# Block products from tile 6 on, the transposed rows of tiles 4 and 5 by way of HBM, and a new written order, in an attention and MLP kernel

## The chip, the cores and the metric

The kernel runs on one core of a Trainium2 chip. Its time is the device time of one execution in microseconds (us). Three runs of the kernel before took 357.02, 357.13 and 357.69 us; the median is 357.13 us.

## The reference

Two stages follow one another. The first is attention over 4 batches, 8 heads, 768 positions of width 64; each query sees the keys less than 16 positions away and, of every block of 32 keys, one summary (the maximum of the keys, the mean of the values):

```python
k_sum = k.reshape(B, H, nb, 32, D).max(axis=3)
v_sum = v.reshape(B, H, nb, 32, D).mean(axis=3)
scores_l = where(abs(i - j) < 16, scale * q @ k.T, -1e9)
scores_s = scale * q @ k_sum.T + log(32)
a = softmax(concat(scores_l, scores_s))
x = a @ concat(v, v_sum)
```

The second works on the 3072 rows of x, with 512 inputs and 1024 hidden values:

```python
h = x @ w_in
solu = h * softmax(h)
ln = (solu - mean) / sqrt(var + 1e-6) * g_ln
out = ln @ w_out
```

## The kernel before

The 3072 rows are 24 tiles of 128. A tile of the second stage needs its attention first, in which the query windows of two neighbouring tiles share loads. Each tile then runs through these steps, many of which stand side by side in the program for different tiles:

- TensorE (PE) makes scores `s`; VectorE (DVE) adds the mask and takes the maximum (L695), ScalarE (ACT) takes the exponential `e` and its sum `z` (L707), adds 1e-9 to `z` (L714), DVE inverts it (L716), and `e<-e,z` multiplies (POOL at L381 or DVE at L380). PE transposes `e` and makes `x` (L796).
- A matrix product in full precision is three products of rounded halves: high by low, low by high, high by high. So `x` is split into `xh` and `xl`, the weights in advance as well.
- `first(t)` (L935) makes `h`: 8 pieces of 3 matmuls of 128x512 for a tile (L949). `first_two(t)` (L960) makes `h` of two tiles at once with seven block products in the place of eight: 7 products of 2 pieces of 3 matmuls, 42 for the pair (L968). It needs combinations of the weights (`ws`, made once) and of the rows of x (`sums`, `combine` in L841 and the lines behind it). The constant `PAIRED` is the first tile that goes this way; `SUMS` and `GATE` are the tiles at which the weights' combinations begin and from which they may.
- The normalised rows `he` have to be transposed for the last product. `turn(t)`: tiles below `FAR_FROM` go through PE (16 transposes `lt<-ident,he`, L739, then a copy and a subtraction from PSUM, L1122); tiles from `FAR_FROM` on are transposed within blocks by DVE (L1074), sent to HBM by one DMA (`farl<-tbl`, L1078), and read back by four (`lt<-farl`, L1084), all issued by SyncE (SP); then `lh` (a cast) and `ll` (a subtraction) are made from SBUF.
- `second(t)` makes `o` with 24 matmuls (L1144); ACT or DVE scales it (L1152, L1154) into `os`, and ACT issues the store (L1156).

The order of the whole program is written out: `Plan` numbers every operation, and the list `ORDER` says in which order they are issued; each engine takes its own in that order. Some operations may run on several engines, with a cost each; the table `OTHERS` (in `Plan`) names those that do not run on their first engine. Costs and landing times give each operation a planned start. These decide one thing only, since the order is fixed: where the plan has PE waiting within the first 80 us, matmuls of a tile of zeros are put in (`keep_up` and `idle`, L1337), called fillers here:

```python
for o in order:
    if o.engine == "pe":
        while at + self.SYNC < min(o.start + o.late, self.FILL):
            at += self.keep_up(at, done)
```

Of the kernel before, what the change touches and what calls it, by code (L numbers as in the profile page):

```python
# [1381 lines left out]
```

## Time and profile before

| | us |
|---|---|
| median of three runs | 357.13 |
| the profiled execution | 357.58 |
| its span, first to last instruction | 355.9 |
| PE busy | 348.6 (98%) |
| DVE busy | 289.7 (81%) |
| ACT busy | 257.3 (72%) |
| POOL busy | 211.4 (59%) |

The mean granted clock of TensorE is 0.997 of the full one. The busy share is an average over the span; a stage in which DVE is busy all the time and one in which it is idle lie behind the 81%. A matmul's row shows the length of one instruction, which overlaps the next; what one costs in a row of them is the length of the row divided by their number.

### The profile page before, as it was taken

To read this page: it belongs to the slowest core of one execution; us is meant where nothing else is said; L and a number is where in the kernel's file an instruction comes from. 1 tells how busy PE (TensorE), PEld (TensorE's weight loads), DVE (VectorE), ACT (ScalarE), POOL (GpSimd) and SP (SyncE) were. 2 spreads that over 40 slices of the span, in tenths; PEclk is the share of its full clock that TensorE was granted. 3 is DMA by queue.
4 is the path that set the end of the run, shared out by engine and by line. 5 is a ranking of instruction groups with operands and counts; after the bars stand their busy time and mean duration, and the time that the engine had idled before them with its cause. 6 is when DMAs were issued, how large, how long until landed. Compare 5 with 4: busy or idle time off the path is not lost.

```text
span 355.9 us, 9340 instructions
## 1 busy us (share of the span) xinstructions
PE 348.6 (98%) x3298; PEld 273.1 (77%) x3298; DVE 289.7 (81%) x960; ACT 257.3 (72%) x773; POOL 211.4 (59%) x342
## 2 busy tenths in 40 slices
PE   7899999999999999999999999999999999999995
PEld 3356576777878887788888888888887888888884
DVE  3999999997888989899798977978988787967220
ACT  3888899974987768668879867785985975736311
POOL 5616558795978777876567277374457373422460
PEclk9999999999999999999999999999999999999998
DMA  7999979047006356285495775375274434355512
GB/s 252 409 409 409 330 288 329 11 136 271 33 3 220 92 196 228 77 266 161 122 361 155 225 246 178 123 228 191 97 240 125 157 116 174 132 172 181 173 60 89
DMA packets 28530, 68.19 MB, mean 192 GB/s; under 512 B 3852, under 2 KB 13324, under 8 KB 26948
## 3 DMA queue, kind: packets, MB, share of 16 engines
q1 hardware_dynamic: 24620, 60.87, 50.7%
q10 hardware_dynamic: 3864, 6.74, 5.2%
q8 instruction: 26, 0.43, 0.5%
q14 instruction: 20, 0.16, 0.1%
HBM read 49.55 MB, written 15.73 MB: 183 GB/s over the span
## 4 chain that ended last, share of the span: by engine, by line
PE 93%; DVE 3%; DMA 2%; SPq 0%; ACT 0%; POOL 0%; issue 0%; ACTq 0%
PE o L1144 38%; PE h L949 13%; PE hu L968 12%; PE x L796 7%; PE hl L968 6%; PE s L674 6%; PE t L739 4%; PE hf L968 3%; DMA kraw<-in_k 2%; PE x L1337 2%; PE vs_ps L561 2%; PE lt L739 1%; DVE e L695 1%; PE vs_ps L574 1%; PE x L788 1%; DVE ksum L541 1%
## 5 line engine op out<-in xcount | busy, mean ns | idle before, releaser
L1144 PE MATMUL o<-w,lh 128*128 128x512 f32 (+1 forms) x400 | 133.4, 388 | 0.0
L1144 PEld LDWEIGHTS o<-w,lh 128*128 128x128 f32 x400 | 74.0, 188 | 15.8 <-DVE he L1039 0.2
L707 ACT ACTIVATE e<-e,nm 128x120 f32<-128x120 f32 x192 | 73.2, 388 | 7.2 <-DVE nm L695 7.2
L1144 PE MATMUL o<-w,ll 128*128 128x512 f32 (+1 forms) x200 | 76.3, 382 | 0.0
L949 PE MATMUL h<-w,xh 128*128 128x512 f32 x128 | 44.9, 404 | 0.0
L695 DVE CUSTOM_DVE_ANT_0 e<-s,mask 128x120 f32<-128x120 f32 x192 | 40.7, 276 | 3.1 <-PE s L674 3.0
L381 POOL TENSOR_TENSOR ll<-lt,lh 128x512 fp32r<-128x512 f32 x19 | 26.7, 1405 | 27.8 <-ACT lh L373 14.7
L1144 PEld LDWEIGHTS o<-w,ll 128*128 128x128 f32 x200 | 37.6, 188 | 6.5
L707 ACT ACTIVATION_READ_ACCUMULATOR e<-e,nm 128x1 f32 x192 | 37.1, 193 | 0.0
L373 ACT COPY at<-t 120x512 f32<-120x512 f32 x40 | 22.0, 588 | 18.7 <-PE t L739 18.1
L381 POOL TENSOR_TENSOR e<-e,z 128x960 f32<-128x960 f32 (+1 forms) x16 | 28.2, 1765 | 8.1 <-DVE z L716 8.0
L1047 POOL TENSOR_SCALAR he<-he,nmu 128x512 f32<-128x512 f32 x24 | 19.2, 801 | 19.2 <-DVE nmu L1042 19.1
L1152 ACT ACTIVATE os<-o,y 128x512 f32<-128x512 f32 (+1 forms) x21 | 14.2, 676 | 21.9 <-PE o L1144 7.5
L949 PEld LDWEIGHTS h<-w,xh 128*128 128x128 f32 x128 | 24.0, 188 | 7.3 <-issue 1.7
L796 PEld LDWEIGHTS x<-at,vt 120*64 120x64 f32 (+1 forms) x768 | 24.3, 138 | 3.4 <-issue 1.8
L796 PE MATMUL x<-at,vt 120*64 120x64 f32 (+1 forms) x768 | 26.4, 224 | 0.0
L1054 ACT ACTIVATE sq<-he 128x1024 bf16<-128x1024 f32 x24 | 25.3, 1056 | 1.0 <-ACT z L714 0.8
L373 ACT CAST lh<-lt 128x512 fp32r<-128x512 f32 x37 | 21.5, 609 | 5.7 <-PE o L1144 5.7
L949 PE MATMUL h<-w,xl 128*128 128x512 f32 x64 | 25.0, 390 | 0.0
L381 POOL TENSOR_TENSOR xl<-sums,xh 128x256 fp32r<-128x256 f32 (+1 forms) x15 | 14.1, 937 | 16.4 <-DVE xh L374 9.2
L1074 DVE STREAM_TRANSPOSE tbl<-he 128x1024 f32<-128x1024 f32 x18 | 22.3, 1238 | 1.0 <-POOL he L1047 0.8
L1031 ACT ACTIVATE he<-hs,hm 128x512 f32<-128x512 f32 x24 | 17.2, 718 | 8.0 <-DVE hm L1021 7.9
(176 smaller groups left out, 837.0 us busy)
## 6 DMA issues: line engine op xcount, KB each, us to landing
vt<-in_v SPq DMA_DIRECT2D x12, 1024.0 KB
farl<-tbl SPq DMA_DIRECT2D x18, 512.0 KB
lt<-farl SPq DMA_DIRECT2D x72, 128.0 KB
kraw<-in_k SPq DMA_DIRECT2D x16, 400.0 KB
out<-os ACTq DMA_DIRECT2D x23, 256.0 KB
qt<-in_q SPq DMA_DIRECT2D x11, 512.0 KB
raw<-in_w_in SPq DMA_DIRECT2D x8, 512.0 KB
raw<-in_w_out SPq DMA_DIRECT2D x8, 512.0 KB
```

Source lines behind the costliest of these rows:

```text
L373: by = {act: lambda: nc.scalar.copy(out=to(), in_=of()), dve: lambda: nc.vector.tensor_copy(out=to(), in_=of()), pool: lambda: nc.gpsimd.t ...
L381: pool: lambda: nc.gpsimd.tensor_tensor(out=to(), in0=a(), in1=b(), op=kind)}
L674: nc.tensor.matmul(scs[i * each].ap[cu * QT:(cu + 1) * QT, j, c:c + ks.shape[-1]], qs.ap[ds, 2 * pp + i, u * QT:(u + 1) * QT], ks, start=T ...
L695: nc.vector.tensor_tensor_reduce(out=e.ap[:, n, :], in0=scs[i * each].ap[:, j, (2 * i + up) * KC:(2 * i + up + 1) * KC], in1=mask[:, mi, : ...
L707: nc.scalar.activation(out=e.ap[:, n, :], in_=e.ap[:, n, :], func=AF.Exp, bias=nm.ap[:, n:n + 1], scale=-1.0, accum_out=z.ap[:, n:n + 1])
L796: nc.tensor.matmul(xp()[j * D:(j + 1) * D, i, qs], vs.ap[:k, u, cs], at.ap[:k, u % 2, n[j] + u // 2, :], start=not apart, stop=not apart o ...
L949: nc.tensor.matmul(hp.ap, a.ap[:, c, ts], w.ap[:, i], start=(c == 0 and n == 0), stop=(c == NKC - 1 and n == 2))
L968: nc.tensor.matmul(to.ap, operand(y, n)[:, c], w(c).ap(i), start=first and c == 0 and k == 0, stop=c == 1 and k == 2, skip_group_check=True)
L1047: op(pool, 0.68, lambda sl=sl: nc.gpsimd.tensor_scalar(out=e.ap[:, sl], in0=e.ap[:, sl], scalar1=nmu.ap, scalar2=1.0, op0=ALU.add, op1=ALU ...
L1054: op(act, 1.05, lambda: nc.scalar.activation(out=sq.ap, in_=e.ap, func=AF.Square, accum_out=ss.ap), r=[e], w=[sq, ss])
L1074: op(dve, 1.17, lambda: nc.vector.transpose(out=tb.ap.rearrange("p (q c a) -> p q c a", q=4, a=32), in_=of().rearrange("p (c q a) -> p q c ...
L1144: nc.tensor.matmul(o.ap[:, cols], a.ap[:, f, :], w.ap[:, i, cols], start=(f == 0 and n == 0), stop=(f == NFC - 1 and n == 2))
```

## The change

- `PAIRED` goes from 8 to 6, so tiles 6 and 7 are a pair in `first_two`; `SUMS` and `GATE` go from 4 to 2, so the combined weights are begun after tile 2.
- `FAR_FROM` goes from 6 to 4: rows of tiles 4 and 5 go by way of HBM.
- Four kinds of small operations get further engines to choose from; some costs of the plan and the planned landing of stores are other numbers.
- `ORDER` and `OTHERS` are new tables; two lines of each stand for them.

```diff
-FAR_FROM = 6
+FAR_FROM = 4
-PAIRED = 8
+PAIRED = 6
-GATE = 4
+GATE = 2
-SUMS = 4
+SUMS = 2
...
-    ORDER = [2, 4, 5, 8, 6, 7, 12, 1, 13, 21, 0, 23, 9, 22, 137, 35, 14, 25, 24, 15, 27, 40, 3, 26, 195, 42, 29, 41,
+    ORDER = [35, 2, 4, 5, 8, 6, 7, 1, 12, 0, 21, 13, 23, 14, 22, 3, 25, 24, 138, 15, 27, 40, 10, 26, 195, 42, 29, 41,
...
-        "dve": (34, 56, 62, 98, 112, 177, 203, 311, 333, 355, 469, 479, 482, 519, 521, 544, 549, 559, 609, 625, 661, 674,
+        "dve": (32, 34, 50, 51, 53, 54, 59, 108, 190, 201, 203, 268, 346, 393, 434, 439, 441, 504, 506, 539, 542, 550,
...
-                out=z.ap[:, ns], in_=z.ap[:, ns], func=AF.Copy, bias=1e-9), w=[(z, i)])
+                out=z.ap[:, ns], in_=z.ap[:, ns], func=AF.Copy, bias=1e-9), w=[(z, i)],
+                alt=[(dve, 0.08, lambda ns=ns: nc.vector.tensor_scalar(
+                    out=z.ap[:, ns], in0=z.ap[:, ns], scalar1=1e-9, scalar2=None, op0=ALU.add)),
+                    (pool, 0.2, lambda ns=ns: nc.gpsimd.tensor_scalar(
+                        out=z.ap[:, ns], in0=z.ap[:, ns], scalar1=1e-9, scalar2=1.0, op0=ALU.add, op1=ALU.mult))])
...
-            split(hi2, lo2, 0, 2, 0, lambda: of(0, 2), [(f, 0), (f, 1)], (((act, 0.52), (dve, 0.34)), lo_ws))
+            split(hi2, lo2, 0, 2, 0, lambda: of(0, 2), [(f, 0), (f, 1)], (((act, 0.52), (dve, 0.34), (pool, 0.7)), lo_ws))
...
-        mul = lambda to, x: op(pool, 0.22, lambda: nc.gpsimd.tensor_tensor(out=to.ap, in0=to.ap, in1=x.ap, op=ALU.mult), r=[x], w=[to])
+        mul = lambda to, x: op(pool, 0.18, lambda: nc.gpsimd.tensor_tensor(out=to.ap, in0=to.ap, in1=x.ap, op=ALU.mult), r=[x], w=[to])
...
-            copy(((act, 0.52), (dve, 0.34)), lambda part=part: part(hi), of, r=[lt], w=[(hi, r)], port=True)
+            copy(((act, 0.52), (dve, 0.34), (pool, 0.75)), lambda part=part: part(hi), of, r=[lt], w=[(hi, r)], port=True)
...
-                out=out[t * P:(t + 1) * P, cols], in_=os.ap[:, cols]), r=[key], nbytes=int(P * 2048 * k))
+                out=out[t * P:(t + 1) * P, cols], in_=os.ap[:, cols]), r=[key], nbytes=int(P * 2048 * k), land=1.2 - 6.55 * k)
```

The lines of the changed kernel have other numbers: L949 becomes L960, L968 becomes L979, L1144 becomes L1155, L739 becomes L750, L714 becomes L721 (on DVE L723), L381 becomes L385, L380 becomes L384, L1152 becomes L1163, L1156 becomes L1167, and L1337 becomes L1348.

Three places show what the tables move. In these rows a name carries its tile (h6 is of tile 6) and, behind the last underscore, the number of its buffer.

On PE, about a third of the way, the kernel before makes `h` of tile 6 piece by piece among the pieces of `o` of tile 2:

```order
L949 MATMUL h6_1_1688<-w3_430,xh1_0_1499 128x512
L949 MATMUL h6_1_1688<-w3_430,xl1_0_1565 128x512
L949 MATMUL h6_1_1688<-w3_430,xh1_0_1499 128x512
L949 MATMUL h6_0_1717<-w0_457,xh1_0_1499 128x512
L949 MATMUL h6_0_1717<-w0_457,xl1_0_1565 128x512
L949 MATMUL h6_0_1717<-w0_457,xh1_0_1499 128x512
L1144 MATMUL o2_1493<-w15_1157,lh2_1329 128x512
```

In the changed kernel the products of the pair (`hl6`, `hu6`, with the combined weights `ws0`, `ws1`, `ws_v`) stand there, and the first matmul of `o` of tile 4 stands behind them:

```order
L979 MATMUL hl6_1838<-ws1_140,xh21_0_1718 128x512
L979 MATMUL hl6_1838<-ws1_140,xl21_0_1816 128x512
L979 MATMUL hl6_1838<-ws1_140,xh21_0_1718 128x512
L979 MATMUL hu6_1739<-ws_v_1618,xh21_0_1718 128x512
L979 MATMUL hu6_1739<-ws_v_1618,xl21_0_1816 128x512
L979 MATMUL hu6_1739<-ws_v_1618,xh21_0_1718 128x512 x2
L979 MATMUL hu6_1739<-ws_v_1618,xl21_0_1816 128x512
L979 MATMUL hu6_1739<-ws_v_1618,xh21_0_1718 128x512
L1155 MATMUL o4_1890<-w8_747,lh4_1835 128x512
```

`h` of tiles 6 and 7 has moved from the single form to the paired one, and `o` of tile 4 stands where it needs rows that have come by way of HBM.

In the kernel before, POOL multiplies `e` of the step 1_0_0 (batch 1, group 0, first half) by the inverted sum:

```order
L603 TENSOR_TENSOR st_v2_0_1_1197<-st_v2_0_1_1197 96x64
L603 TENSOR_TENSOR vacc2_0_160<-st_v2_0_0_1166 96x64
L381 TENSOR_TENSOR e1_0_0_1245<-e1_0_0_1245,z1_0_0_1298 128x960
L1057 TENSOR_TENSOR y1_189<-y1_189,ss1_188 128x1
L607 TENSOR_TENSOR vacc2_0_160<-vacc2_0_160,st_v2_0_1_1197 96x64
```

In the changed kernel DVE adds to `z`, inverts it and multiplies `e` of the same step:

```order
L548 TENSOR_REDUCE ksum1_1_1331<-kraw1_1_917 128x24
L723 TENSOR_SCALAR z1_0_0_1304<-z1_0_0_1304 128x8
L548 TENSOR_REDUCE ksum1_1_1331<-kraw1_1_917 128x24
L727 RECIPROCAL z1_0_0_1304<-z1_0_0_1304 128x8
L816 TENSOR_TENSOR xl0_2_1241<-x0_2_1_1263,xh0_2_1209 128x512
L1053 TENSOR_SCALAR nmu3_195<-s13_181 128x1
L384 TENSOR_TENSOR e1_0_0_1282<-e1_0_0_1282,z1_0_0_1304 128x960
L384 TENSOR_TENSOR ws_own_1071<-w2_459,w3_532 128x512 x2
```

The multiplication has moved from POOL to DVE, the addition to `z` from ACT to DVE, and the combined weights (`ws_own`) stand beside them, a tile pair earlier.

At the end of the program, ACT's last rows before are a scaling of one half of tile 23, one of the whole of tile 22, and three stores in a row:

```order
L1152 ACTIVATE os23_5098<-o23_5036,y23_4993 128x256
L1152 ACTIVATE os22_5101<-o22_4995,y22_4999 128x512
L1156 DMA out_0<-os23_5098 128x256
L1156 DMA out_0<-os22_5101 128x512
L1156 DMA out_0<-os23_5098 128x256
```

In the changed kernel ACT scales both halves of tile 23 and stores each behind its scaling; tile 22 is scaled by DVE (not in these rows), and its store is the last:

```order
L1163 ACTIVATE os23_5089<-o23_5052,y23_4968 128x256
L1167 DMA out_0<-os23_5089 128x256
L1163 ACTIVATE os23_5089<-o23_5048,y23_4968 128x256
L1167 DMA out_0<-os23_5089 128x256
L1167 DMA out_0<-os22_5106 128x512
```

One store stands behind the last scaling, where two stood before. PE's last three matmuls are those of tile 22 in both.

## Rows read from the trace of the kernel before

**Rows 1.** the page: busy time, share of the span, instructions of each engine.

```profile
PE 348.6 (98%) x3298; PEld 273.1 (77%) x3298; DVE 289.7 (81%) x960; ACT 257.3 (72%) x773; POOL 211.4 (59%) x342
```

**Rows 2.** waits of PE: engine, line, what it waited for; us, times, longest.

```profile
PE vs_ps L1337 <- DVE zero L398: 1.2, 1, 1.2
PE s L674 <- DVE ksum L541: 1.2, 2, 0.6
PE t L739 <- POOL e L381: 0.4, 1, 0.4
```

**Rows 3.** windows of the core: stretch, its us, busy us (instructions) of each engine.

```profile
10.00:80.00 70.00, 69.46 (x770) 46.18 (x771) 67.77 (x233) 62.72 (x186) 46.12 (x61) 1.00 0.79 288
80.00:90.00 10.00, 10.00 (x106) 7.87 (x106) 7.13 (x21) 5.15 (x17) 5.82 (x11) 1.00 0.69 243
```

**Rows 4.** the chain that ended last: start, us, engine, operation, count.

```profile
79.83 5.46 PE h L949 x24
```

**Rows 5.** timeline of PE, 63 to 66 us: start, us, line, operation, count.

```profile
64.06 0.71 PE L739 MATMUL lt<-ident,he 64*128 64x64 f32 x16
64.70 0.50 PE L1144 MATMUL o<-w,lh 128*128 128x512 f32 x1
```

**Rows 6.** timeline of PE, 29.5 to 36 us: fillers and what follows them.

```profile
29.83 0.82 PE L1337 MATMUL x<-zero 128*128 128x512 bf16 x3
30.57 0.47 PE L949 MATMUL h<-w,xh 128*128 128x512 f32 x1
...
33.80 1.47 PE L1337 MATMUL x<-zero 128*128 128x512 bf16 x6
34.92 0.58 PE L949 MATMUL h<-w,xh 128*128 128x512 f32 x1
```

**Rows 7.** line of the fillers: count, ns min/median/max, first and last start in us.

```profile
L1337 PEld LDWEIGHTS <-zero x46: 95/98/151, 1.2 to 60.8; 128*128 128x128 bf16 x46
```

**Rows 8.** one line of DVE by form: count, ns min/median/max, first and last start.

```profile
L380 DVE TENSOR_TENSOR ll<-lt,lh x17: 676/686/1773, 149.9 to 342.7; 128x512 fp32r<-128x512 f32 x17
...
L380 DVE TENSOR_TENSOR e<-e,z x10: 793/1154/1165, 13.1 to 290.1; 128x960 f32<-128x960 f32 x9, 128x480 f32<-128x480 f32 x1
...
L380 DVE TENSOR_TENSOR w<-cv,w x6: 680/684/692, 20.9 to 34.8; 128x512 fp32r<-128x512 f32 x6
L380 DVE TENSOR_TENSOR ws_own<-w,w x5: 642/683/684, 85.3 to 113.4; 128x512 f32<-128x512 f32 x5
```

**Rows 9.** groups of DVE: shapes, count, busy us, mean ns, idle before them.

```profile
L380 DVE CUSTOM_DVE_ANT_0 cv<-cv 128x1024 uint16<-128x1024 uint16 x12 | 8.0, 684 | 0.2 <-ACT cv L477 0.2
...
L472 DVE TENSOR_SCALAR cv<-raw 128x512 int32<-128x512 int32 x16 | 7.3, 477 | 0.0
...
L716 DVE RECIPROCAL z<-z 128x8 f32<-128x8 f32 (+1 forms) x26 | 5.0, 191 | 6.4 <-ACT z L714 6.3
```

**Rows 10.** timeline of the core, 342 to 345 us: POOL and DVE at once.

```profile
342.42 1.41 POOL L381 TENSOR_TENSOR ll<-lt,lh 128x512 fp32r<-128x512 f32 x1 [1.45 <-DVE lh L374]
...
342.71 1.67 DVE L380 TENSOR_TENSOR ll<-lt,lh 128x512 fp32r<-128x512 f32 x1
```

**Rows 11.** timeline of SP, 125 to 137 us: send and last fetches of tile 6.

```profile
126.91 0.33 SPq L1078 DMA_DIRECT2D farl<-tbl  x1
...
132.84 0.89 SPq L1084 DMA_DIRECT2D lt<-farl  x2
```

**Rows 12.** timeline of the core's end, from 350.8 us.

```profile
351.28 0.39 PE L1144 MATMUL o<-w,lh 128*128 128x512 f32 x1
351.75 0.69 ACT L1152 ACTIVATE os<-o,y 128x512 f32<-128x512 f32 x1 [0.22 <-PE o L1144]
351.83 1.46 ACTq L1156 DMA_DIRECT2D out<-os  x3
```

**Rows 13.** the scaling on DVE: count, ns min/median/max, first and last start.

```profile
L1154 DVE TENSOR_SCALAR os<-o,y x4: 483/748/752, 185.9 to 350.8; 128x512 f32<-128x512 f32 x3, 128x256 f32<-128x256 f32 x1
```

**Rows 14.** the stores' issues on ACT's queue: count, ns, first and last start.

```profile
L1156 ACTq DMA_DIRECT2D out<-os x25: 338/339/1195, 74.1 to 352.9; - x25
```

More of the change, by code (lines that the diff above doesn't have):

```diff
@@ L99 @@
     SYNC = 0.16
-    ORDER = [2, 4, 5, 8, 6, 7, 12, 1, 13, 21, 0, 23, 9, 22, 137, 35, 14, 25, 24, 15, 27, 40, 3, 26, 195, 42, 29, 41,
[93 rows of a table removed]
-    OTHERS = {
-        "dve": (34, 56, 62, 98, 112, 177, 203, 311, 333, 355, 469, 479, 482, 519, 521, 544, 549, 559, 609, 625, 661, 674,
[4 rows of a table removed]
-        "pool": (70, 105, 109, 110, 116, 137, 179, 195, 234, 236, 239, 241, 243, 260, 306, 308, 370, 401, 466, 467, 471,
[3 rows of a table removed]
-        "act": (431, 509, 592, 760, 779, 920, 938, 939, 1077, 1218, 1237, 1376, 1515, 1646, 1664, 1665, 1747, 1766),
+    ORDER = [35, 2, 4, 5, 8, 6, 7, 1, 12, 0, 21, 13, 23, 14, 22, 3, 25, 24, 138, 15, 27, 40, 10, 26, 195, 42, 29, 41,
[95 rows of a table added]
+    OTHERS = {
+        "dve": (32, 34, 50, 51, 53, 54, 59, 108, 190, 201, 203, 268, 346, 393, 434, 439, 441, 504, 506, 539, 542, 550,
[4 rows of a table added]
+        "pool": (56, 68, 114, 177, 179, 184, 186, 195, 232, 234, 236, 239, 241, 243, 244, 266, 308, 316, 326, 328, 329,
[4 rows of a table added]
+        "act": (166, 167, 223, 290, 291, 374, 375, 461, 462, 526, 527, 625, 626, 644, 645, 785, 803, 804, 943, 944, 963,
+            1241, 1242, 1260, 1261, 1401, 1538, 1557, 1558, 1669, 1688, 1689, 1771, 1789),
     }
@@ L502, in split_w_out @@
         op(act, 0.61, lambda: nc.scalar.activation(out=hl.ap[:, 0], in_=w(), func=AF.Copy, scale=gs),
-           r=[(st, 0), g_b], w=[(hl, 0)])
+           r=[(st, 0), g_b], w=[(hl, 0)], alt=[(dve, 0.36, lambda: nc.vector.tensor_scalar(
+                out=hl.ap[:, 0], in0=w(), scalar1=gs, scalar2=None, op0=ALU.mult)),
+                (pool, 0.72, lambda: nc.gpsimd.tensor_scalar(
+                    out=hl.ap[:, 0], in0=w(), scalar1=gs, scalar2=1.0, op0=ALU.mult, op1=ALU.mult))], port=True)
         op(dve, 0.66, lambda: nc.vector.scalar_tensor_tensor(
@@ L847, in combine @@
                r=[xb, (f, 0)], w=[(f, 1)])
-            split(hi, lo, 1, 1, 0, lambda: of(1), [(f, 1)], (((act, 0.3), (dve, 0.2)), lo_hs))
+            split(hi, lo, 1, 1, 0, lambda: of(1), [(f, 1)], (((act, 0.3), (dve, 0.2), (pool, 0.4)), lo_hs))
         else:
@@ L856, in combine @@
                r=[xb, (f, 1)], w=[(f, 2)])
-            split(hi2, lo2, 0, 2, 0, lambda: of(0, 2), [(f, 0), (f, 1)], (((act, 0.52), (dve, 0.34)), lo_ws))
-            split(hi2, lo2, 2, 1, 0, lambda: of(2), [(f, 2)], (((act, 0.3), (dve, 0.2)), lo_hs))
+            split(hi2, lo2, 0, 2, 0, lambda: of(0, 2), [(f, 0), (f, 1)], (((act, 0.52), (dve, 0.34), (pool, 0.7)), lo_ws))
+            split(hi2, lo2, 2, 1, 0, lambda: of(2), [(f, 2)], (((act, 0.3), (dve, 0.2), (pool, 0.4)), lo_hs))
     class Sub:
@@ L1055, in solu @@
             out=sq.ap, in_=e.ap, func=AF.Square, accum_out=ss.ap), r=[e], w=[sq, ss])
-        mul = lambda to, x: op(pool, 0.22, lambda: nc.gpsimd.tensor_tensor(out=to.ap, in0=to.ap, in1=x.ap, op=ALU.mult), r=[x], w=[to])
-        op(pool, 0.25, lambda: nc.gpsimd.tensor_scalar(
+        mul = lambda to, x: op(pool, 0.18, lambda: nc.gpsimd.tensor_tensor(out=to.ap, in0=to.ap, in1=x.ap, op=ALU.mult), r=[x], w=[to])
+        op(pool, 0.2, lambda: nc.gpsimd.tensor_scalar(
             out=ss.ap, in0=ss.ap, scalar1=1.0 / DF, scalar2=1e-6, op0=ALU.mult, op1=ALU.add), w=[ss])
@@ L1063, in solu @@
         mul(ss, y)
-        op(pool, 0.25, lambda: nc.gpsimd.tensor_scalar(
+        op(pool, 0.2, lambda: nc.gpsimd.tensor_scalar(
             out=ss.ap, in0=ss.ap, scalar1=-0.5, scalar2=1.5, op0=ALU.mult, op1=ALU.add), w=[ss])
@@ L1189, in attn_then_solu @@
         load_v_rows(1, i)
-    op(pool, 3.1, selector_q, w=[sel_q])
+    op(pool, 3.8, selector_q, w=[sel_q])
     for f in range(NFC):
```

203 rows, old and new, of tables (ORDER, OTHERS) are left out of this document.

## The prediction

> **What bounds the kernel now.** I read the page's busy times first, then PE's waits, then the windows by stretch, and the chain of waits last. PE is busy 348.6 of 355.9 us, DVE, the next, 289.7 [rows 1]. PE's waits are short: 1.2 us once at the start, and behind it 1.2 us in two and 0.4 us in one [rows 2]. So a PE instruction taken away is time won as long as nothing else becomes late, and the question of this change is whether something does. The average hides one stretch: from 10 to 80 us DVE is busy 67.77 of 70 us, idle for 2.23, with ACT at 62.72 and POOL at 46.12; from 80 to 90 us DVE is idle for 2.87 [rows 3]. In the early stretch PE and DVE bound the kernel together. PE looks busy there partly because of fillers: 46 of them, all before 61 us [rows 7]. They are no work; they stand where the plan has PE waiting. Behind 80 us PE alone is the bound.
>
> **PE's own work.** Tiles 6 and 7 take 42 matmuls of 128x512 in the place of 48: 6 fewer. In the chain 24 such matmuls take 5.46 us [rows 4], 0.2275 us each, so 6 x 0.2275 = 1.37 us go. Tiles 4 and 5 lose 16 transposes each on PE; a group of 16 starts at 64.06 and the next matmul at 64.70 [rows 5], so 2 x 0.64 = 1.28 us go. The changed kernel's program holds 54 fillers, 8 more. Six fillers take 34.92 - 33.80 = 1.12 us, 0.19 each; three take 30.57 - 29.83 = 0.74 us, 0.25 each [rows 6]. I take the middle, 0.22: 8 x 0.22 = 1.76 us come, with 1.5 and 2.0 as ends. Twelve of the 54 stand in one row ahead of a single group of scores, more than in any row before. PE's work by itself changes by -1.37 - 1.28 + 1.76 = -0.89 us.
>
> **What DVE gets in the early stretch.** Ahead of the first matmul of `h` of tile 5 (half 1), DVE's list has three more `e<-e,z` (6 for 3; two of the three are half tiles of 128x480), four more additions to `z`, two more `w<-cv,w` and two more `ws_own<-w,w`, and on the other side four fewer `cv<-raw` and two fewer of the custom `cv<-cv`. By the rows: 2 x 0.79 + 1.15 = 2.74 us for `e`, 2 x 0.684 + 2 x 0.683 = 2.73 us for the weights [rows 8]; for the additions, which the trace does not show on DVE, the reciprocal of the same shape, 4 x 0.19 = 0.76 us; off go 4 x 0.477 + 2 x 0.684 = 3.28 us [rows 9]. The smaller moves (a few copies and casts each way) about cancel. So DVE has some 2.74 + 2.73 + 0.76 - 3.28 = 2.95 us more to do there, against 2.23 us of idle time up to 80 us and another 2.87 us up to 90 [rows 3]. If all idle time could be used, 2.95 - 2.23 = 0.7 us would be left over for PE to wait, and the added fillers, 1.76 us of PE time, stand for waits of that kind already. Then nothing is added. If none of the idle time can be used and the fillers stand elsewhere, all 2.95 us come on top. Below nothing: of the waits in [rows 2] those behind the start, 1.6 us, may go in the new order, since they hang on DVE and POOL. I take +0.3 us, near the lower end, because the nearest row, DVE from 10 to 80 us with 97% busy, goes with only 1.6 us of waits; both ends are kept for the range.
>
> **The other engines.** POOL loses work on balance: `e<-e,z` falls from 16 to 10, `ll` from 19 to 12, while it takes 12 half-tile casts of `lh` and 6 additions to `z`; ACT loses 19 additions to `z` and gains 16 of the `he<-he,nmu`. Both have idle time of 7 and 24 us even between 10 and 80 us [rows 3], so I put these at nothing; PE's work hides them, and if that cover fails the wait is counted with DVE's above. `STREAM_TRANSPOSE` and the splits of tiles 4 and 5 fall behind the stretch in which DVE is full.
>
> **The round trip of tiles 4 and 5.** It adds two sends and eight fetches to SP's queue and a wait of `o` of tile 4 for its rows. In the trace the send of tile 6 is issued at 126.91 and its last two fetches end at 132.84 + 0.89 = 133.73 us [rows 11]: 6.8 us. In the changed program 69 matmuls of 128x512 stand on PE between the transposition of tile 4 and the first matmul of its `o`, 69 x 0.2275 = 15.7 us, and 44 of them (10.0 us) stand behind the last fetch. Behind that come a landing, two casts and two subtractions of 0.68 us on DVE or up to twice that on POOL [rows 8, 10]. That fits with some us to spare; SP has nothing queued behind the fetches that PE needs within those us but loads of later tiles. I put it at nothing; if the trip were as long again, 13.6 us, it would still about fit.
>
> **The end.** The last matmul ends at 351.28 + 0.39 = 351.67. ACT scales tile 22 from 351.75 to 352.44, and of the three stores queued [rows 12] the last is issued at 352.9 [rows 14], 1.23 us behind the matmul. In the changed program DVE scales tile 22, 0.748 us [rows 13], and its store is the only one behind it: 0.08 for the hand-over as before, 0.75, and the 0.1 or so of a start of the queue, 0.93 us. That wins 0.3 us. Ends: 0.6 us won, if what the last three stores move together also shortens the landing, and 0.3 us lost, one issue of 0.34 us [rows 14], if the store of the half tile stands in the way.
>
> **The sum.** -0.89 + 0.3 - 0.3 = -0.89 us, against the profiled execution of 357.58 us (355.9 of span and 1.68 around it): 356.69. That execution lay 0.45 us above the median of the runs, 357.13; from the median the forecast is 356.24, so 356.2 us. A measurement of this kernel can tell about 0.2% from no change, 0.7 us; faster means under 356.42, slower over 357.84.
>
> **A rule weighed against it.** Near the end a subtraction on POOL takes 1.41 us from 342.42, and the same on DVE, begun beside it at 342.71, takes 1.67 [rows 10], where its line's median is 0.686 [rows 8]: 1.0 us lost by running at once. The Trainium skill, "SBUF — State Buffer", section "Who interferes with whom", says that DVE and GpSimd share one pair of ports as an exclusive lock, and that a DVE instruction with two inputs from SBUF contends with a GpSimd instruction that reads SBUF. The trace agrees in this one place. By that rule each product that goes to DVE in the full stretch may also be held up, and the sum would come out as in the third rival.
>
> **Rivals.** First, more is won: the new order also removes the 1.6 us of waits, or the fillers are at 0.19 each and the stores win 0.6: -1.37 - 1.28 + 1.52 - 0.6 = -1.73 us, 355.4 us. For it speaks that PE is the bound after 80 us whatever else happens; against it, that DVE gets more to do in just the stretch where it is full.
>
> Second, no change: the fillers stand at other places than DVE's lateness, so that the 0.7 us that DVE can't hide and a part of the idle time that can't be used, 1.3 us together, come on top: -0.89 + 1.3 - 0.3 = +0.1 us, 357.2 us. For it speaks that DVE's idle time of 2.23 us is spread over 70 us; against it, that the order may put the added work where it is idle.
>
> Third, slower: DVE and POOL in one another's way before 80 us. Ahead of `h` of tile 5 DVE gets seven more instructions with two inputs from SBUF (three `e`, two `w`, two `ws_own`), and POOL is busy 46.12 of 70 us there [rows 3], so by chance 7 x 0.66 = 4.6 of them would meet one. At 1.0 us each [rows 10], not all under an idle stretch, I price it at 2.5 us: -0.89 + 2.5 - 0.3 = +1.3 us, 358.4 us. It decides from two such meetings that nothing hides (1.9 us of them bring the time over 357.84). Against it: POOL has fewer products of that kind itself (three fewer `e<-e,z` in that stretch).
>
> That the change doesn't do what it says is excluded by the program: the matmuls, the transposes and the fillers are counted from it.
>
> **How the numbers follow.** The forecast has 0.42, by itself 355.6 to 356.9; the first rival 0.12, the second 0.22, the third 0.24. Of the forecast 0.34 lies under 356.42 and 0.08 within; the first rival is faster; the second is within, but 0.02 of it slower; the third is slower but for 0.02. Faster 0.46, the same 0.30, slower 0.24. The range that leaves out 2 in 10 goes from 354.9, below the first rival, to the third's 358.4.
>
> **What would show it.** Right: single `h` at L960 with 144 matmuls for 192, the paired products with 378 for 336, `lt` on PE 32 fewer; 54 fillers of about 0.22 us; PE's listed waits no longer than 3 to 4 us in sum; DVE idle for under 1 us of 10 to 80; no wait of `o` of tile 4 for `lh` or `ll`; some 3.9 us from the last matmul to the end. Wrong: waits of PE for DVE's `e`, `hm` or `z` before 80 us that exceed 2 us, `ll` or `e` on DVE well over their medians, or PE waiting at `o` of tile 4.

## The result, and the profile after

The changed kernel takes 360.01 us (median of 12 executions, 358.69 to 363.17); the kernel before, run beside it, 357.45 us (356.83 to 357.92). The ratio is 1.0078, 95% interval 1.0058 to 1.0097: slower, by 2.6 us (0.8%) where 0.9 us less was forecast. The profiled execution took 359.18 us, its span 357.5, against 357.58 and 355.9 before; it is the second shortest of the twelve.

The page's busy times of the changed kernel:

```profile
PE 348.5 (97%) x3268; PEld 271.4 (76%) x3268; DVE 303.9 (85%) x987; ACT 265.1 (74%) x770; POOL 185.8 (52%) x337
```

Against [rows 1] DVE has gained 14.2 us and POOL lost 25.6. PE is as busy as before though it does less: a part of its busy time must be waiting that its busy share doesn't show. The waits of PE (engine, line, what it waited for; us, times, longest):

```profile
PE h L960 <- DVE he L1050: 1.4, 1, 1.4
PE vs_ps L1348 <- DVE zero L402: 1.2, 1, 1.2
PE s L681 <- DVE ksum L548: 0.6, 1, 0.6
```

The first is new against [rows 2], and the only one listed between 85 and 115 us, where the kernel before has none. The windows of the changed kernel, in the columns of [rows 3] (stretch, its us, then PE, PEld, DVE, ACT, POOL):

```profile
10.00:80.00 70.00, 69.10 (x773) 45.85 (x765) 67.15 (x237) 65.16 (x187) 36.44 (x48) 1.00 0.79 295
70.00:80.00 10.00, 10.00 (x125) 7.47 (x124) 9.82 (x36) 9.06 (x24) 6.53 (x8) 1.00 0.36 110
80.00:90.00 10.00, 9.68 (x108) 7.33 (x108) 10.00 (x15) 7.03 (x18) 6.41 (x10) 1.00 0.09 19
90.00:100.00 10.00, 8.64 (x59) 6.79 (x54) 9.93 (x34) 7.67 (x26) 8.29 (x14) 1.00 0.01 2
100.00:110.00 10.00, 10.00 (x140) 7.89 (x139) 9.97 (x36) 9.78 (x26) 6.41 (x11) 1.00 0.54 180
110.00:120.00 10.00, 10.00 (x57) 7.81 (x56) 9.91 (x32) 8.33 (x32) 3.45 (x7) 1.00 0.91 288
```

and the same view of the kernel before, behind the stretch shown in [rows 3]:

```profile
90.00:100.00 10.00, 10.00 (x111) 8.14 (x107) 8.30 (x30) 9.24 (x29) 7.65 (x8) 1.00 0.08 28
100.00:110.00 10.00, 10.00 (x105) 8.11 (x102) 9.90 (x48) 8.96 (x37) 8.62 (x16) 1.00 0.23 62
110.00:120.00 10.00, 10.00 (x139) 8.00 (x139) 8.25 (x19) 6.04 (x19) 7.44 (x11) 1.00 0.68 219
```

Up to 80 us DVE is no fuller than before (67.15 us of 70, for 67.77). From 80 us on it was idle at times before (7.13 busy of 10 in [rows 3], then 8.30, and 8.25 behind 110); after, it is full for 40 us on end. In 80 to 90 us it has only 15 instructions in ten full microseconds, where [rows 3] shows 21 in 7.13: they are larger ones, and 1.6 us of the ten are time over their usual lengths (below).

**A measure for the rest of the text.** PE's busy time hides short waits, so I count its lateness: the start of a matmul, less the time that all PE instructions ahead of it take by themselves (each form at its spacing in unbroken stretches). That own work sums to 338.06 us in the kernel before and 337.23 after: -0.83, where -0.89 was forecast. Other fair choices of the spacings move this difference to -0.7 and the lateness differences by up to 0.3 us. Lateness in us, at six places of the profiled executions:

| | 80 | 95 | 110 | 150 | 210 | 350 us |
|---|---|---|---|---|---|---|
| before | 10.9 | 11.4 | 11.8 | 13.4 | 13.3 | 13.3 |
| after | 10.5 | 13.3 | 13.7 | 15.4 | 15.5 | 15.9 |
| after, run again (e7) | 10.2 | 13.0 | 13.4 | 15.1 | 15.4 | 20.3 |
| stores early (e9) | 10.6 | 13.4 | 13.8 | 15.5 | 15.6 | 16.0 |
| POOL quiet (e5) | 11.1 | 11.6 | 12.0 | 12.8 | 13.6 | 14.0 |
| both (e13) | 11.1 | 11.6 | 12.0 | 12.8 | 13.0 | 13.5 |
| before, POOL quiet (e12) | 11.4 | 11.8 | 12.3 | 13.4 | 13.3 | 13.3 |

Nothing is lost against the kernel before up to 80 us. From 80 to 95 the changed kernel loses 2.8 us, the one before 0.5. The later loss, in e7, comes behind 210 us. The profiled difference adds up: -0.83 of work, +2.6 of lateness (15.9 - 13.3), and -0.1 at the end (4.07 us from PE's last matmul to the end of the span, for 4.19): +1.7 us, as the spans show (357.5 and 355.9).

**The place of the first loss.** The timeline of the changed kernel (start, us, engine, line, operation):

```profile
88.92 1.27 POOL L610 TENSOR_TENSOR st_v<-st_v 96x512 f32<-96x512 f32 x1
89.08 1.28 DVE L378 COPY kw<-ksum 128x192 f32<-128x192 f32 x1
...
90.14 1.35 POOL L385 TENSOR_TENSOR ws<-ws_own,ws 128x512 fp32r<-128x512 f32 x1
...
90.28 1.43 DVE L1039 TENSOR_TENSOR hm<-hm 128x1 f32<-128x1 f32 x1
...
91.75 0.69 ACT L1042 ACTIVATE he<-h,hm 128x512 f32<-128x512 f32 x1 [3.19 <-DVE hm L1039]
```

`hm` is a subtraction on one element per partition, and takes 1.43 us; the rows of its line (count, ns min/median/max) have a median of 0.158:

```profile
L1039 DVE TENSOR_TENSOR hm<-hm x6: 145/158/1430, 37.9 to 101.8; 128x1 f32<-128x1 f32 x6
...
L378 DVE COPY kw<-ksum x6: 245/247/1284, 43.2 to 263.6; 128x192 f32<-128x192 f32 x6
...
L723 DVE TENSOR_SCALAR z<-z x13: 163/502/893, 12.1 to 291.7; 128x8 f32<-128x8 f32 x11, 128x4 f32<-128x4 f32 x2
```

The two in the timeline end about their own length behind the end of the POOL instruction beside them: POOL's `st_v` ends at 90.19, `kw` at 90.36; POOL's `ws` at 91.49, `hm` at 91.71. ACT had waited 3.19 us for that `hm`, and through ACT's `he` and DVE's `he` (L1050) it is what PE waits for at 94.51. Between 70 and 110 us such excess over the usual length of the same form sums to 6.3 us in the changed kernel and 1.0 in the one before.

The Trainium skill, "SBUF — State Buffer", section "Who interferes with whom", says that the pair of ports that DVE shares with GpSimd is an exclusive lock, that a DVE instruction with two inputs from SBUF contends with a GpSimd instruction that reads SBUF, that a copy or scalar operation in a fast mode contends too, and that a `tensor_reduce` on trn2 never does. The rows agree on the first three: a meeting costs the rest of the POOL instruction, whatever the size of DVE's own. On the last they say little: the reductions at L1037 stay between 0.63 and 0.69 us, but they read `h` from PSUM.

**The place of the second.** There are two `os` buffers, so a scaling waits for the store of the tile two before. ACT's order in the changed kernel has the store of tile 7 at row 228 and the scaling of tile 9, which needs the same buffer, at 233; before they stood at 214 and 225, and in the trace before 13.6 us lie between them (195.09 and 208.71) and the scaling doesn't wait for the store. ACT's rows in the profiled execution, then in a second one (e7):

```profile
203.73 0.35 ACTq L1167 DMA_DIRECT2D out<-os  x1
...
210.24 0.69 ACT L1163 ACTIVATE os<-o,y 128x512 f32<-128x512 f32 x1 [1.51 <-DMA out<-os]
```

```profile
204.24 0.34 ACTq L1167 DMA_DIRECT2D out<-os  x1
...
213.69 0.69 ACT L1163 ACTIVATE os<-o,y 128x512 f32<-128x512 f32 x1 [4.39 <-DMA out<-os]
```

The store lands 6.5 us after its issue in one execution and 9.4 in the other, and in the second PE stands still for it:

```profile
PE o L1155 <- ACT os L1163: 2.4, 1, 2.4
```

In the first execution the DMA engines are full just then (DMA share is the last column but one):

```profile
206.00:210.00 4.00, 4.00 (x19) 3.33 (x18) 3.96 (x9) 2.72 (x12) 1.62 (x2) 1.00 1.00 408
```

In the second the share is 0.96 in the same stretch and 0.29 from 210 to 214, and the store still lands only at 213.7; why it took 3 us longer was not found.

**The end.** As in [rows 12], of the changed kernel:

```profile
353.07 0.39 PE L1155 MATMUL o<-w,lh 128*128 128x512 f32 x1
353.31 1.37 ACTq L1167 DMA_DIRECT2D out<-os  x2
353.56 0.75 DVE L1165 TENSOR_SCALAR os<-o,y 128x512 f32<-128x512 f32 x1 [8.15 <-issue]
```

The last store is issued at 354.34, 0.88 us behind the last matmul, as forecast (0.93, for 1.23 before); from there to the end of the span it takes 3.2 us, for 3.0 before, so of the 0.35 us won 0.1 is left.

### The profile page after: what moved, and what is told of

Its sections match the earlier page's. It is cut to its first block, busy times and chain, and to the rows that moved or that the text cites. A ratio compares the mean times of both kernels' runs of the same rounds, so it can differ in the third digit from the quotient of the medians.

```text
span 357.5 us, 9335 instructions
## 1 busy us (share of the span) xinstructions
PE 348.5 (97%) x3268; PEld 271.4 (76%) x3268; DVE 303.9 (85%) x987; ACT 265.1 (74%) x770; POOL 185.8 (52%) x337
## 4 chain that ended last, share of the span: by engine, by line
PE 59%; DVE 12%; ACT 4%; issue 3%; ACTq 0%
PE o L1155 28%; PE hu L979 13%; PE hl L979 6%; PE x L807 4%; PE s L681 3%; PE hf L979 3%; PE t L750 2%; DVE e L702 2%; DVE ws_own L384 2%; ACT e L714 2%; DVE he L1050 1%; DVE e L384 1%; ACT he L1062 1%; DVE hm L1037 1%; DVE ll L1133 1%
## 5 line engine op out<-in xcount | busy, mean ns | idle before, releaser
L1155 PE MATMUL o<-w,lh 128*128 128x512 f32 (+1 forms) x400 | 132.7, 387 | 0.0
L1155 PEld LDWEIGHTS o<-w,lh 128*128 128x128 f32 x400 | 74.0, 188 | 15.8 <-issue 0.5
L714 ACT ACTIVATE e<-e,nm 128x120 f32<-128x120 f32 x192 | 73.2, 386 | 6.8 <-DVE nm L702 6.1
L1155 PE MATMUL o<-w,ll 128*128 128x512 f32 (+1 forms) x200 | 76.3, 382 | 0.0
L1155 PEld LDWEIGHTS o<-w,ll 128*128 128x128 f32 x200 | 37.6, 188 | 6.6
L714 ACT ACTIVATION_READ_ACCUMULATOR e<-e,nm 128x1 f32 x192 | 36.7, 191 | 0.0
L960 PE MATMUL h<-w,xh 128*128 128x512 f32 x96 | 33.5, 403 | 1.4 <-DVE he L1050 1.4
L1062 ACT ACTIVATE he<-he,nmu 128x512 f32<-128x512 f32 x34 | 23.9, 720 | 6.4 <-DVE nmu L1053 6.4
L1042 ACT ACTIVATE he<-hs,hm 128x512 f32<-128x512 f32 x27 | 19.5, 722 | 11.0 <-DVE hm L1032 11.0
L1085 DVE STREAM_TRANSPOSE tbl<-he 128x1024 f32<-128x1024 f32 x20 | 24.7, 1237 | 1.7 <-ACT he L1062 0.9
L377 ACT CAST lh<-lt 128x512 fp32r<-128x512 f32 x27 | 15.9, 608 | 11.8 <-PE o L1155 11.0
L384 DVE TENSOR_TENSOR ll<-lt,lh 128x512 fp32r<-128x512 f32 x28 | 18.4, 688 | 6.6 <-POOL lh L379 3.8
L385 POOL TENSOR_TENSOR xl<-sums,xh 128x256 fp32r<-128x256 f32 (+1 forms) x17 | 16.4, 967 | 14.1 <-ACT xh L377 9.4
L960 PEld LDWEIGHTS h<-w,xh 128*128 128x128 f32 x96 | 18.0, 188 | 7.0 <-DVE he L1050 2.1
L385 POOL TENSOR_TENSOR e<-e,z 128x960 f32<-128x960 f32 (+1 forms) x10 | 17.4, 1740 | 9.5 <-DVE z L727 8.6
L1050 DVE SCALAR_TENSOR_TENSOR he<-hs,hz,he 128x512 f32<-128x512 f32 x27 | 21.4, 805 | 0.2
L681 PE MATMUL s<-kw,qt 64*64 64x120 f32 x704 | 21.5, 267 | 0.1
```

The source lines that it names most:

```text
L377: by = {act: lambda: nc.scalar.copy(out=to(), in_=of()), dve: lambda: nc.vector.tensor_copy(out=to(), in_=of()), pool: lambda: nc.gpsimd.t ...
L384: by = {dve: lambda: nc.vector.tensor_tensor(out=to(), in0=a(), in1=b(), op=kind), pool: lambda: nc.gpsimd.tensor_tensor(out=to(), in0=a() ...
L385: pool: lambda: nc.gpsimd.tensor_tensor(out=to(), in0=a(), in1=b(), op=kind)}
L681: nc.tensor.matmul(scs[i * each].ap[cu * QT:(cu + 1) * QT, j, c:c + ks.shape[-1]], qs.ap[ds, 2 * pp + i, u * QT:(u + 1) * QT], ks, start=T ...
L714: nc.scalar.activation(out=e.ap[:, n, :], in_=e.ap[:, n, :], func=AF.Exp, bias=nm.ap[:, n:n + 1], scale=-1.0, accum_out=z.ap[:, n:n + 1])
L960: nc.tensor.matmul(hp.ap, a.ap[:, c, ts], w.ap[:, i], start=(c == 0 and n == 0), stop=(c == NKC - 1 and n == 2))
```

## The experiments

My theory after the first profile: DVE's new work, put where POOL adds up the combined weights, runs into POOL, and the time lost is DVE waiting for POOL's reads ("meetings"). The rival: DVE simply has too much to do there, and any place for it would cost as much ("work"). Later a second fault was added to both: stores placed too late.

**e1, e2, e3: one side of the meetings made short, or taken away.**

```diff
-                out=o.ap[:n, :w], in0=x.ap[:n, :w], in1=x.ap[:n, w:2 * w], op=ALU.add),
+                out=o.ap[:n, :v], in0=x.ap[:n, :v], in1=x.ap[:n, w:w + v], op=ALU.add),
```

> The changed kernel, but the halving additions that GpSimd makes for the block means of the values (st_v) take 8 columns in place of 512 to 128, so most of the means of two batches are left out; the instructions and their order stay. In the trace of the changed kernel VectorE loses 6.3 us in 79 to 110 us on ten instructions that run far over their usual length, each beside a GpSimd instruction, four of them beside st_v. Theory of meetings (VectorE and GpSimd hold one another up, and VectorE is what PE waits for there): 2 to 3.5 us less than the changed kernel's 360.0, so 356.5 to 358, and a smaller spread of the runs. Theory of work (VectorE simply has more instructions than fit between 60 and 130 us, GpSimd has idle time): under 0.5 us of change, 359.5 to 360.3.

Measured: 361.04 us (360.45 to 362.07), ratio 1.0106 (1.0087 to 1.0124). Neither: DVE met the next POOL instruction instead, and the overlong DVE time between 70 and 110 us stayed at 6.8 us. Making one of many POOL instructions short is no test of meetings.

```diff
-        by = {dve: lambda: nc.vector.tensor_tensor(out=to(), in0=a(), in1=b(), op=kind),
+        cut = (lambda x: x[:, :, :16]) if kind == ALU.mult else (lambda x: x)
+        by = {dve: lambda: nc.vector.tensor_tensor(out=cut(to()), in0=cut(a()), in1=cut(b()), op=kind),
```

> The changed kernel, but where VectorE multiplies e by the inverted sum it takes 16 of 120 columns, so most of these products are left out on VectorE; all else stays. Each gets about 0.9 us shorter, four of them stand between 78 and 113 us. Both theories (work, meetings) say that VectorE is what PE waits for between 78 and 130 us: 2.5 to 4 us less than 360.0, so 356 to 357.5. If PE is late for another reason (the trip of the rows by HBM, ACT's chain), it stays within 0.7 us of 360.0.

Measured: 359.08 us (358.03 to 360.59), ratio 1.0052 (1.0033 to 1.0071). That is 0.9 us less than the changed kernel, where both theories wanted 2.5 to 4. Lateness at 150 us is 1.1 us less than after, so the products are a part of the load; 2.3 us are then lost behind 205 us, where a store takes 8.1 us to land (issued at 203.52, and the scaling begins at 211.63).

e3 puts all 26 additions to `z` on ACT:

```diff
-L723 TENSOR_SCALAR z0_0_0_167<-z0_0_0_167 128x4
+L721 ACTIVATE z0_0_0_167<-z0_0_0_167 128x4
```

> The changed kernel, but all 26 additions to z run on ACT, as they could only do before (13 come from VectorE, 6 from GpSimd). In the trace of the changed kernel two of them take 0.69 and 0.89 us on VectorE between 80 and 100 us, where the shortest takes 0.17, both beside a GpSimd instruction. Theory of meetings: 0.8 to 1.6 us less, 358.4 to 359.2. Theory of work: 0.17 us each, so at most 0.5 us less, 359.5 or more. If ACT's place in the order is worse for z, no gain or a loss.

Measured: 360.59 us (359.88 to 364.92), ratio 1.0107 (1.007 to 1.0144). No gain: with thirteen short instructions off DVE the overlong time between 70 and 110 us is as large as before, on other instructions that meet POOL, and lateness at 150 us is 16.3.

**e4: the rows of tiles 4 and 5 by HBM alone, in the kernel before.**

```diff
-FAR_FROM = 6
+FAR_FROM = 4
```

> The kernel before with FAR_FROM 4 alone: the rows of tiles 4 and 5 by HBM, at the places that they have in the changed order, all else in the order and on the engines of before. PE loses 2 x 0.64 = 1.28 us, VectorE gets two block transposes of 1.24 us between 80 and 115 us, where it is idle for about 5 us. Forecast's step (the trip costs nothing): 356.2, 1.3 us less than 357.45. Theory of work: between that and no change, 356.2 to 357.4. A trip that is late for o of tiles 4 or 5: 358 or more.

Measured: 377.72 us, ratio 1.0568 (1.0551 to 1.0584). It says nothing about the part: in the order that I merged, DVE's instruction on the fetched rows stood ahead of work that PE needed, and everything behind it waited too:

```profile
PE s L675 <- DVE ll L1123: 14.3, 1, 14.3
```

In the changed kernel's own order the trip causes no wait of PE, as forecast. e4 shows only what an order costs that doesn't cover the trip.

**e5 and e12: POOL made quiet, in the changed kernel and in the one before.** The additions and subtractions on POOL for the combined weights write a constant and read nothing; `st_v` is cut as in e1. The same edit in both:

```diff
-              pool: lambda: nc.gpsimd.tensor_tensor(out=to(), in0=a(), in1=b(), op=kind)}
+              pool: lambda: nc.gpsimd.memset(to().bitcast(F32), 0.0) if blank else nc.gpsimd.tensor_tensor(out=to(), in0=a(), in1=b(), op=kind)}
```

> The changed kernel with GpSimd's reads taken out where VectorE is late: its additions and subtractions for the combined weights (ws_own, ws, ws_v, w1s) become fills with zeros, which read nothing, and the halving additions of the block means take 8 columns; so the combined weights and the means are wrong there, while the instructions' number, order and engines stay. The shortening of the means alone left VectorE with as many overlong instructions in 70 to 110 us as before, so it told nothing of the meetings. Theory of meetings: the overlong instructions of VectorE in 70 to 110 us, 6.3 us over their usual lengths in the changed kernel, go under 1.5 us, and PE, late by 15.4 us against its own work at 150 us in the changed kernel's profile, is late by 13.0 to 13.8 (13.4 in the kernel before). Theory of work: VectorE stays busy without a break until 130 us and PE's lateness at 150 us stays above 14.8.

> The kernel before with the same reads of GpSimd taken out (combined weights filled with zeros, means short), as a control: VectorE's overlong instructions in 70 to 110 us are only 1.0 us there and VectorE has idle time behind them. Theory of meetings: 0 to 0.7 us less, 356.5 to 357.2, so that the changed kernel without these reads and the kernel before without them are within 0.5 us of one another. If the quiet GpSimd wins 2 us or more here too, it shortens something else than the meetings.

Measured: e5 357.10 us (356.27 to 358.59, and one execution of 362.2), ratio 0.9993 (0.9981 to 1.0006); e12, the control, 356.86 (356.34 to 357.57), ratio 0.9985 (0.9977 to 0.9994). So the edit takes 2.9 us off the changed kernel's median and 0.6 off the other's, a difference of 2.3 us. The place of the first loss, in e5:

```profile
88.66 0.52 POOL L385 MEMSET ws<- 128x512 f32 x1
88.78 0.52 DVE L378 COPY kw<-ksum 128x192 f32<-128x192 f32 x1
...
89.22 0.14 DVE L1040 TENSOR_TENSOR hm<-hm 128x1 f32<-128x1 f32 x1
...
89.39 0.69 ACT L1043 ACTIVATE he<-h,hm 128x512 f32<-128x512 f32 x1 [1.37 <-DVE hm L1040]
```

`hm` is back at 0.14 us, the `he` behind it starts 2.4 us sooner, and the excess between 70 and 110 us is 0.7 us. DVE has the same instructions as in the changed kernel, so "work" alone falls. The edit also makes POOL faster (0.52 for 1.35 us), so it doesn't tell reads from the mere length of what POOL does; and it could bring weights sooner, but what PE waited for at 94.51 was `he`, not a weight.

**e10** is e5's kernel once more, one execution; its stores stand as in the changed kernel, whatever its label says.

> One more look at the changed kernel with GpSimd's reads taken out (combined weights filled with zeros, means short), for the spread: its eleven runs had two of 358.6 and 362.2 beside 356.3 to 357.5. Theory of late stores: PE's lateness is near 13 us at 200 us and grows, if at all, at 205 to 230 us, by 0.5 to 5 us.

Measured: 356.66 us. ACT waits 1.9 us for a store in it, so the late stores are still there, and cost little this time.

**e6: fewer fillers**, 18 for 54.

```diff
-    COLD, FILL = 6.9, 80.0
+    COLD, FILL = 6.9, 14.0
```

> The changed kernel with fillers up to 14 us alone: 18 in the place of 54. If fillers are PE time on the path, as the forecast's sum has them, 36 x 0.22 = 7.9 us less. If they only stand where PE waits for VectorE, the same time within 0.7 us of 360.0, unless the granted clock falls in the waits: then slower, by up to some us.

Measured: 361.99 us (360.09 to 362.37), ratio 1.0121 (1.01 to 1.0141). The waits grow where fillers stood: from 27 to 33 us PE is busy 2.91 us of 6, where the changed kernel has 6.00. Then the granted clock falls, the only time in the run: it is 0.50 of the full one, the lower level of 1.2 GHz, from 33 to 36 us, and 0.82 on average from 36 to 40. So the fillers as a whole are no loss; what the 8 added ones alone cost was not tried. The page's row of the clock (40 slices of 9 us), and PE's longest wait:

```profile
PEclk9996999999999999999999999999999999999999
```

```profile
PE s L681 <- DVE nm L702: 3.1, 1, 3.1
```

**e7: the changed kernel again.** No edit.

> The changed kernel once more, for its spread and for a second profile beside the first, which came from a run of 359.18 us while the median of twelve was 360.0: in one kernel of the first set PE also lost 2 us at 217 to 223 us, where VectorE took 3.85 us for a subtraction (xl) that takes 0.41. Theory of meetings: VectorE's overlong instructions are others in each run, so PE's lateness after 150 us differs by 1 to 3 us between the two profiles. Theory of work: the lateness has the same course within 0.5 us.

Measured: 360.19 us (359.03 to 363.66), ratio 1.0096 (1.0063 to 1.0129); the profiled execution was the longest, 363.66. I had expected the meetings to differ from run to run: wrong. The excess per 10 us from 70 us on is 0.9, 1.6, 2.6, 1.2, the same as before. What differs is the landing of the store shown above, which led to e9 and e11.

**e8: two products of `e` back on POOL.**

```diff
+L385 TENSOR_TENSOR e1_0_0_1282<-e1_0_0_1282,z1_0_0_1304 128x960
+L385 TENSOR_TENSOR e1_0_1_1448<-e1_0_1_1448,z1_0_1_1487 128x960
```

> The changed kernel, but the two products e<-e,z of the steps 1_0_0 and 1_0_1 run on GpSimd, as they did before; in its trace they stand on VectorE at 84.5 and 99.2 us and take 1.15 and 1.48 us. Theory of work: 2.3 to 2.6 us less for VectorE in its full stretch, PE's lateness at 150 us falls from 15.4 by 1.5 to 2.3, the time is 358 to 358.6. Theory of meetings: GpSimd is busy 3.6 us longer there and holds up as much as it frees: within 0.7 us of 360.0.

Measured: 359.27 us (358.46 to 360.69), ratio 1.0063 (1.0045 to 1.0082). Lateness at 150 us falls from 15.4 to 14.4: a part, as with e2. That is less than the 1.5 to 2.3 of "work", and the time is nearer to what "meetings" wanted (within 0.7 us of 360.0) than to the 358 to 358.6 of "work".

**e9 and e11: the stores.** e9 is the changed kernel with the stores of seven tiles moved soon behind their scalings (here tile 7's, with ACT's row numbers); e11 is the kernel before with three stores placed late. Tile 7's stands two rows ahead of the scaling that needs its buffer, where the changed kernel has five, so e11 shows the mechanism and not its size there.

```diff
-228 L1167 DMA out_0<-os7_2922 128x512
+214 L1168 DMA out_0<-os7_2922 128x512
```

> The changed kernel, but the stores of tiles 4, 7, 8, 12, 13, 14 and 17 are issued soon behind their scaling. There are two buffers os; in the changed order the store of tile 7 stands on ACT's queue shortly ahead of the scaling of tile 9, which needs its buffer, and in both profiles of the changed kernel ACT waits there for the store to land, 1.5 and 4.4 us; PE's lateness between 210 and 230 us grows by 0.3 in the one and 4.8 us in the other. Theory of late stores: that loss goes, the runs spread over less than 1.5 us, the median is 358.6 to 359.3. If the spread has another cause, the median stays at 360.0 to 360.2 and the spread at 4 to 5 us.

> The kernel before, but the stores of tiles 4, 7 and 17 stand on ACT's queue as shortly ahead of the scaling that needs their buffer as they do in the changed order. Theory of late stores: the time rises by 0.5 to 3 us, 357.8 to 360.4, and its spread to 2 us or more. If the landing doesn't matter there, 357.2 as before, within 0.4.

Measured: e9 359.39 us (358.26 to 359.82), ratio 1.0049 (1.0032 to 1.0065), and no wait of ACT for a store; 0.6 us less than the changed kernel, and no execution over 359.82. Median and spread (1.56 us) miss the theory's limits, 359.3 and 1.5, by 0.1 us; the other cause, 360.0 or more with 4 to 5 us of spread, is out. e11 360.84 us (359.67 to 362.68), ratio 1.0097 (1.0071 to 1.0123): three late stores by themselves cost the kernel before 3.4 us. Its waits of ACT and of PE:

```profile
ACT os L1153 <- DMA out<-os: 5.7, 1, 5.7
```

```profile
PE o L1145 <- ACT os L1153: 1.9, 1, 1.9
```

**e13: both faults taken away**, e5's edit and e9's together.

> The changed kernel with both faults taken away: POOL's additions and subtractions for the combined weights write a constant and read nothing (so that part of the result is left out), and the stores of seven tiles stand soon behind their scalings. If the two faults are all of the loss: no wait of ACT for a store, DVE held up by less than 1 us between 70 and 110 us, 356.3 us, within 355.9 to 356.8, some 0.5 us less than the kernel before with the same quiet POOL (356.86). If a third loss remains that neither touches: 357 us or more, as with the quiet POOL alone (357.10).

Measured: 356.87 us (356.38 to 357.85), ratio 0.999 (0.9978 to 1.0002). In its windows DVE has a little idle time, though it is nearly as full as after, and PE is not kept waiting:

```profile
80.00:90.00 10.00, 10.00 (x113) 7.93 (x111) 9.84 (x25) 8.26 (x24) 5.92 (x16) 1.00 0.10 21
90.00:100.00 10.00, 10.00 (x84) 8.07 (x83) 9.40 (x31) 9.81 (x32) 3.81 (x14) 1.00 0.01 2
```

Its span is 355.1 us, 0.8 less than before, and PE's lateness ends at 13.5 (13.3 before): the forecast's gain, in that execution. The median stands 0.6 under the kernel before and level with the control e12 (356.86). Seven of its executions lie at 356.4 to 356.9, five at 357.7 to 357.9, and what parts them was not found. The median misses both ranges that were set: 0.1 us over the one without a third loss, and 0.1 under the 357 that spoke for one. So the two faults carry the 2.6 us by which the changed kernel is slower (3.1 us less without them, where the quiet POOL alone takes 0.6 off the kernel before). That the 0.9 us won in PE's work and at the end then come out as a gain is shown by the one profile, not by the medians: beside the control nothing is won, and where that part goes stays open.

**e14 and e15: other orders.** The products and the rows by HBM as in the changed kernel, POOL reading as before, ordered anew with `z` counted among the instructions that POOL holds up, and the stores planned as before. The table of engines is new too (DVE adds to `z` less often, POOL makes more of the products `e`), so these two are not a change of order alone.

```diff
-                alt=[(dve, 0.08, lambda ns=ns: nc.vector.tensor_scalar(
+                port=True, alt=[(dve, 0.17, lambda ns=ns: nc.vector.tensor_scalar(
...
-                out=out[t * P:(t + 1) * P, cols], in_=os.ap[:, cols]), r=[key], nbytes=int(P * 2048 * k), land=1.2 - 6.55 * k)
+                out=out[t * P:(t + 1) * P, cols], in_=os.ap[:, cols]), r=[key], nbytes=int(P * 2048 * k))
```

> The same division of the work as in the changed kernel (42 products for a tile pair from tile 6 on, rows of tiles 4 and 5 by HBM), in a new order in which the additions to z count as instructions that POOL can hold up and stores are planned as in the kernel before. POOL reads as before. If the meetings can be planned away: DVE held up by less than 3 us between 70 and 110 us (6.3 in the changed kernel), PE's lateness at 110 us under 12.8, 356.8 us, within 356.2 to 357.8. If the division of the work itself fills DVE there, whatever the order: lateness at 110 us of 13.3 or more and 358.5 us or more.

> As the run before it, with a second order found from another start. If the meetings can be planned away: 356.9 us, within 356.2 to 358. If they depend on phases that no plan knows, the two orders differ by 1 us or more between them, though planned alike. If the division of the work fills DVE, both are at 358.5 us or more.

Measured: e14 372.64 us (371.63 to 373.38), ratio 1.0423 (1.0405 to 1.0441); e15 367.44 (366.52 to 367.7), ratio 1.0275 (1.026 to 1.029). Both fail, and 5 us apart. In e14 one DVE addition is held up through POOL's next four instructions:

```profile
102.77 4.17 DVE L384 TENSOR_TENSOR ws<-ws_own,ws 128x512 fp32r<-128x512 f32 x1
```

```profile
102.88 1.29 POOL L385 TENSOR_TENSOR ws_own<-ws_own,w 128x512 f32<-128x512 f32 x1
104.12 0.33 POOL L379 COPY kw<-ksum 128x192 f32<-128x192 f32 x1
104.42 1.28 POOL L385 TENSOR_TENSOR ws_own<-w,w 128x512 f32<-128x512 f32 x1
105.67 0.71 POOL L385 TENSOR_TENSOR xl<-sums,xh 128x256 fp32r<-128x256 f32 x1
```

PE's lateness in e14 goes from 17.6 to 23.4 there. In e15 the excess stays low (1.7 us between 80 and 110) and lateness at 110 us is 12.5, under the changed kernel's 13.7, as that theory wanted; it then loses 3 us to 190 us and 3.8 behind it, and at the end the scaling of tile 22 on DVE begins only at 360.13, 2.2 us behind PE's last matmul, since the store of tile 20, whose buffer it needs, is issued only at 357.98; the end is some 7 us long for 4. A good order for this division was not found: no version here that computes the whole result is faster than the kernel before, and whether one exists stays open.

## Why the prediction was wrong

**PE's own work** was right: -0.83 us for -0.89. The changed trace has 144 single matmuls of `h`, 32 fewer `lt`, and 54 fillers. Whether the 8 added fillers are a cost of 1.76 us, as the sum has them, no run shows.

**What DVE gets in the early stretch** is the step that failed. I asked whether DVE's added 2.95 us fit into its idle time up to 80 us, took +0.3 us for them, and looked no further. The stretch was the wrong one. Up to 80 us DVE is idle for 2.85 us of 70, a little more than before, and PE's lateness is 0.4 us less; the loss stands at 80 to 95 us. So the sign that was set, waits of PE before 80 us, could not show it. The idle time that [rows 3] shows at 80 to 90 us is what I let absorb the surplus; in the new order DVE runs full through it to 120 us, and a surplus that meets POOL there is not counted by adding up usual durations. So "Behind 80 us PE alone is the bound" doesn't hold in the new order. In its place: 2.3 us more lateness than before is made between 80 and 95 us, by DVE instructions waiting out POOL's. (The smaller moves on DVE's list do not cancel either: there are two more `kw`, three more `w` and one more `sums` for one `he` and one `lh` less. It didn't matter, as DVE isn't fuller up to 80 us.)

**The other engines at nothing** failed with it. POOL does less in sum, and less from 80 to 120 us as well (24.55 us of 40 busy, for 29.52), but its additions for the combined weights (`GATE` and `SUMS` begin them after tile 2) now meet a DVE without idle time. I also wrote that transposes and splits of tiles 4 and 5 fall behind the stretch in which DVE is full: DVE is full until 120 us, and the transposition of tile 4 (102.23 us) lies in it, that of tile 5 (120.99) just behind.

**The third rival** had the mechanism and, by luck, a near size: DVE and POOL in one another's way, 358.4 us. It had the place wrong (before 80 us), and it counted only `e`, `w` and `ws_own` as instructions that can be held up. Of the longest holds between 70 and 110 us, two on `ws_own` (1.2 and 0.9 us over the usual length) are of its kind; `hm` on 128x1 (1.3) and a copy of 128x192 (1.0), which stand in the chain that PE waits for, are not. I gave it 0.24, against 0.42 for the forecast, because POOL has fewer products itself; that balance of work says nothing on phases.

**The places of the stores** were never priced. I looked at the last stores only, and not at the other ones, which the new order moves as well. They add some 0.6 to 0.8 us to the median (359.39 without them, 360.01 and 360.19 with), and most of the spread: the upper end of the changed kernel's executions is 363.

**The round trip** was right: no wait of PE for `lh` or `ll` of tile 4. **The end** had the right sign: 0.1 us won, for 0.3; the issue came as forecast, but the landing took 0.2 us longer.

Put together: -0.83 + 2.6 - 0.1 = +1.7 us between the two profiled executions. The medians differ by 0.9 us more, since the changed kernel's profiled execution lies 0.8 us under its median and the other's 0.1 over; for that part stores that land later are the likely cause (with the stores early, e9's profiled execution is its median).

## What to carry to other kernels

When work moves from POOL to DVE, price it by what POOL does at the same time, not by DVE's idle time: an instruction of 0.15 us can cost 1.4. Look for idle time behind the place where work is added as well as in it, and ask what now fills the idle time that kept the bound engine supplied. When a table changes the order of everything, compare the places of all transfers that free a buffer, and count how far behind each the instruction stands that needs it.
